# Attention with a key/value cache: 160 instead of 320 rows of wo go through the first five DMA engines

## Chip, core and metric

The kernel runs on one core of a Trainium2 chip. The metric is the device time of one execution in microseconds (us), lower being better. Before the change it is 189.44 us, the median of four runs (188.45, 188.66, 190.21 and 192.01 us).

A core has a matrix engine (PE, whose weight loads are listed apart as PEld), a vector engine (DVE), a scalar engine (ACT), GpSimd (POOL) and a synchronising engine (SP), which here issues the transfers. Sixteen DMA engines carry the transfers out.

## What is computed

```python
q = (x @ wq).reshape(B, Sq, Hq, Dh).transpose(0, 2, 1, 3)
k = jnp.repeat(k_cache, rep, axis=1)
v = jnp.repeat(v_cache, rep, axis=1)
scores = jnp.einsum("bhqd,bhkd->bhqk", q, k) * (Dh ** -0.5)
o = jnp.einsum("bhqk,bhkd->bhqd", softmax(scores), v)
return o.transpose(0, 2, 1, 3).reshape(B, Sq, Hq * Dh) @ wo
```

B is 8, Sq 4, D 512, Hq 32, Hkv 8 (so rep is 4), Sk 2048 and Dh 128; all in bf16. The caches k and v are 33.5 MB each (8 x 8 x 2048 x 128 x 2 bytes), wq and wo 4.2 MB each, and the output is 32 KB. The kernel reads 75.5 MB once and does little arithmetic on each byte.

## The kernel before

**Units.** Work goes in 32 units: four pairs of key/value heads (`p`) times eight batches (`b`), `units[u]`. A unit has 1 MB of k and 1 MB of v, each in one transfer into a tile of 128 partitions x 8 KB (`load_k`, L118, and `load_v`, L128). There are 7 k buffers and 6 v buffers. The loop at L488 takes step `n`: it transposes the keys of unit n on PE (L215) and copies them out on DVE and ACT (L216), computes the scores (L286) and the exponentials (L296) of unit n-1, transposes the probabilities on DVE (L306), and multiplies unit n-2 with its v (L343 for the last 20 units, L381 for pairs of the first 12).

**Transfers.** All loads are issued by SP, in the order of the list `loads` that is built at L153 to L163. The order begins: k of unit 0, wq (4 MB), x, then for u = 1, 2, ...: one `wo_e` transfer (as long as u is at most 8), k of unit u, v of unit u-2. `load_ready` (L165) issues from this list at the end of a step, as far as there are buffers. SP's transfers carry eight landing semaphores in rotation, so that transfer number m is issued when number m-8 has landed; a transfer has landed when the last of its DMA engines has. A tile of 128 partitions is spread evenly: each of the 16 DMA engines carries 8 partitions. A transfer of 5 partitions uses five DMA engines with one partition each. They are called the first five here.

**wo.** The 4096 rows of `wo` are used in four parts of 1024 rows, one for each `p`. Parts 1 to 3 are loaded at the end in eight transfers (L148), 128 partitions each. Part 0 is divided among three tiles (L52):

- `wo_e`: NE x WE = 40 x 8 = 320 rows. A partition holds 8 rows (8 KB). They come in eight transfers of five partitions each (`load_wo_e`, L133; 40 KB a transfer): transfers 0 to 3 fill partitions 0 to 19, transfers 4 to 7 partitions 32 to 51. The tile has 64 partitions, and the ones that no row fills are set to zero on POOL first (L178).
- `wo_m`: 128 x WM = 640 rows, five to a partition, and `wo_n`: the last WN = 64 rows, one to a partition. They are loaded near the end, just ahead of v of the last unit (L140 to L144).

**The output projection.** The attention output of part 0 is brought into the order of these rows: `to_tokens(0)` transposes it to token-major and copies it to `nat_sb` (L438 to L442; the columns for `wo_e` are copied as two blocks of 256, with columns of other rows filling the partitions that are zero in `wo_e`), and `to_wo_rows(0)` transposes it back, one transpose for each row slot (L459 to L463), into `oE`, `oM` and `oN`. `project(p, r0, n)` (L468) accumulates in PSUM (`out_ps`), two matmuls for each row slot. The `wo_e` slots are done in steps 14 to 17 (L531), the `wo_m` and `wo_n` slots one step before the last unit (L533). After the last unit come `to_tokens(2)`, `to_wo_rows(2)` and the projection of parts 1 to 3 (L536 to L543), then the copy to `out_sb` (L545) and two stores.

The tiles `pad0` and `pad` hold nothing: they only set where the tiles after them lie in SBUF.

Of the kernel before, what the change touches and what calls it, by code (L numbers as in the profile page):

```python
# [8 lines left out]
BF16 = mybir.dt.bfloat16  # L9
# [5 lines left out]
def kernel(  # L15
# [9 lines left out]
    nc = tc.nc  # L25

    B, Sq, D = x.shape
# [4 lines left out]
    T = B * Sq  # L32
# [8 lines left out]
    HP = 2 * rep  # L41
# [7 lines left out]
    DH = D // 2  # L49


    NE, WE, WM, WN = 40, 8, 5, 64  # L52
    assert NE * WE + 128 * WM + WN == HP * 128
    AX = mybir.AxisListType.X
    ADD = mybir.AluOpType.add
# [2 lines left out]
    const = ctx.enter_context(tc.tile_pool(name="const", bufs=1))  # L58
# [13 lines left out]


    pad0 = const.tile([128, 192], BF16, name="pad0")
    wo_e = const.tile([64, WE, D], BF16, name="wo_e")
    wo_n = const.tile([WN, D], BF16, name="wo_n")
    wo_m = const.tile([128, WM, D], BF16, name="wo_m")
    x_sb = const.tile([T, D], BF16, name="x_sb")
# [11 lines left out]
    oT = [const.tile([128, HP, len(ps), B, Sq], BF16, name=f"oT{ps[0]}") for ps in groups]  # L90
    out_sb = const.tile([2 * T, DH], BF16, name="out_sb")
    oP12 = const.tile([128, WR, 2, T], BF16, name="oP12")
    nat_sb = const.tile([2 * T, HP * 128 + 24 * WE], BF16, name="nat_sb")
    oP3 = const.tile([128, WR, T], BF16, name="oP3")
    oP = [None, oP12[:, :, 0, :], oP12[:, :, 1, :], oP3[:, :, :]]
    oE = const.tile([64, WE, T], BF16, name="oE")
    oM = const.tile([128, WM, T], BF16, name="oM")
    oN = const.tile([WN, T], BF16, name="oN")
    ident = const.tile([128, 128], BF16, name="ident")
# [3 lines left out]

    fold = const.tile([128, 2, 2, NQ], FP32, name="fold")
    ones = const.tile([128, 128], FP32, name="ones")
    pad = const.tile([128, 64], BF16, name="pad")
    probs = [const.tile([128, C, 2, HQ], BF16, name=f"probs{i}") for i in range(3)]

    units = [(p, b) for p in range(G2) for b in range(B)]
# [22 lines left out]

    def load_wo_e(i):  # L133

        hi, m = divmod(i, 4)
        rows = wo[: NE * WE, :].rearrange("(q r) j -> q r j", r=WE)
        a, b = hi * 32 + m, hi * NE // 2 + m
        nc.sync.dma_start(wo_e[a : a + 17 : 4, :, :], rows[b : b + 17 : 4, :, :])

    def load_wo_m():  # L140
        nc.sync.dma_start(wo_n[:, :], wo[HP * 128 - WN : HP * 128, :])
# [10 lines left out]
    nc.sync.dma_start(x_sb[:, :], x.flatten_outer_dims())  # L152
    loads = []  # L153
    for u in range(NU + KA):
        if 1 <= u <= 8:
            loads.append(("e", u - 1))
        if 0 < u < NU:
            loads.append(("k", u))
        if u == NU + KA - 2:
            loads.append(("m", 0))  # L160
        if u >= KA - 1 and u - KA + 1 < NU:
            loads.append(("v", u - KA + 1))
    loads.reverse()  # L163

    def load_ready(nk, nv):  # L165

        while loads:
            kind, u = loads[-1]
            if kind in "em":
                loads.pop()  # L170
                load_wo_e(u) if kind == "e" else load_wo_m()
                continue
            if u >= (nk + KB if kind == "k" else nv + VB):
                return
            loads.pop()
            (load_k if kind == "k" else load_v)(u)
# [6 lines left out]
    for e in range(2):  # L183
        for g in range(2):
            nc.vector.tensor_copy(
                out=pick[:, e, g, :], in_=ident[:, :].rearrange("d (k e) -> d e k", e=2)[:, e, :]
            )
    nc.vector.memset(q_bd[:, :, :, :, :, :, :], 0.0)
    for t in probs:
# [3 lines left out]
        out=by_q[:, :, :],  # L193
        in_=ident4[:, :].rearrange("p (g c q) -> p g q c", g=2, q=HQ),
# [4 lines left out]
    for c in range(2):  # L199
        nc.vector.tensor_copy(  # L200
            out=fold[:, c, :, :],
            in_=ident4[:, :].rearrange("p (u c q) -> p c u q", u=2, c=2)[:, c, :, :],
# [28 lines left out]
    for half in range(2):  # L231
        psq = psum_s.tile([4 * T, rep * Dh], FP32, tag="s", name="psq")
        for r in range(R):
            for k in range(4):
                n = (half * 4 + k) * rep * Dh
# [15 lines left out]
        for k in range(4):  # L251
            nc.vector.tensor_copy(  # L252
                out=qT_all[:, half * 2 + k // 2, :, k % 2 * rep : (k % 2 + 1) * rep, :],
                in_=qtp[:, :, k, :, :].rearrange("d h b s -> d b h s"),
            )
    for pp in range(0, G2, 2):
        for e in range(2):
# [9 lines left out]
            for g in range(2):  # L267
                rows = slice(g * 64, (g + 1) * 64)
                (nc.scalar.copy if g else nc.vector.tensor_copy)(
                    out=q_bd[rows, pp : pp + 2, e, :, :, g, :].rearrange("d p b g q -> d p (b g) q"),  # L270
                    in_=pse[rows, :, :, :, :].rearrange("d p b g q -> d p (b g) q"),
# [150 lines left out]
    nats = {}  # L422

    def to_tokens(n):
        rows = len(groups[n]) * T
        nat = psum_l.tile([rows, HP, 128], BF16, tag="l", name="nat")
        for h in range(HP):
            nc.tensor.transpose(
                nat[:, h, :], oT[n][:, h, :, :, :].rearrange("d p b s -> d (p b s)"), ident[:, :]
            )  # L430
        flat = nat[:, :, :].rearrange("t h d -> t (h d)")
        nats[n] = nat_sb[:rows, : HP * 128 + (n == 0) * 24 * WE]
        if n > 0:
            nc.vector.tensor_copy(out=nats[n][:, :], in_=flat)
            return

        w = 32 * WE
        nc.vector.tensor_copy(out=nats[0][:, :w], in_=flat[:, :w])  # L438
        nc.vector.tensor_copy(
            out=nats[0][:, w : 2 * w], in_=flat[:, NE // 2 * WE : NE // 2 * WE + w]  # L440
        )
        nc.vector.tensor_copy(out=nats[0][:, 2 * w :], in_=flat[:, NE * WE :])  # L442

    def to_wo_rows(n):
        rows = len(groups[n]) * T
        if n > 0:
            perm = psum_l.tile([128, WR, rows], BF16, tag="l", name="perm")
            by_row = nats[n][:, :].rearrange("t (q r) -> t r q", r=WR)
            for r in range(WR):
                nc.tensor.transpose(perm[:, r, :], by_row[:, r, :], ident[:rows, :rows])  # L450
            to = oP3[:, :, :] if n == 2 else oP12[:, :, :, :].rearrange("q r p t -> q r (p t)")
            nc.vector.tensor_copy(out=to, in_=perm[:, :, :])
            return

        perm = psum_l.tile([128, WE + WM + 1, T], BF16, tag="l", name="perm")
        w = 64 * WE
        by_row = nats[0][:, :w].rearrange("t (q r) -> t r q", r=WE)
        for r in range(WE):
            nc.tensor.transpose(perm[:64, r, :], by_row[:, r, :], ident[:T, :T])  # L459
        by_row = nats[0][:, w : w + 128 * WM].rearrange("t (q r) -> t r q", r=WM)  # L460
        for r in range(WM):
            nc.tensor.transpose(perm[:, WE + r, :], by_row[:, r, :], ident[:T, :T])
        nc.tensor.transpose(perm[:WN, WE + WM, :], nats[0][:, w + 128 * WM :], ident[:T, :T])  # L463
        nc.vector.tensor_copy(out=oN[:, :], in_=perm[:WN, WE + WM, :])
        nc.vector.tensor_copy(out=oE[:, :, :], in_=perm[:64, :WE, :])
        nc.vector.tensor_copy(out=oM[:, :, :], in_=perm[:, WE : WE + WM, :])

    def project(p, r0, n):  # L468
# [19 lines left out]
    for n in range(NU + A):  # L488
        w = n - A
# [16 lines left out]
        if w >= 0:  # L506
            p, b = units[w]
            if p in (1, 3) and b == 1:
                to_tokens(p // 2)
            if w >= NU - NS:  # L510
                values(w)
                if w % 2 == 0:
                    norms(w)
                finish(w)
            elif w % 2 == 1:
                values2(w - 1)
            if p in (1, 3) and b == 2:
                to_wo_rows(p // 2)
# [14 lines left out]
        if w == NU - 2:  # L533
            project(0, WE, WM + 1)

    to_tokens(2)  # L536
    project(1, 0, 4)
    to_wo_rows(2)
    project(1, 4, 4)
    project(2, 0, 4)  # L540
# [37 lines left out]
```

The softmax here doesn't subtract the row's maximum and nothing guards it: scores larger than these inputs give would overflow.

## Time and profile before

| | |
|---|---|
| median of four runs | 189.44 us (188.45 to 192.01) |
| the profiled execution's own time | 190.21 us |
| its span in the profile | 188.4 us |
| PE, PEld, DVE busy | 76%, 61%, 70% of the span |
| ACT, POOL busy | 33%, 2% |
| SP's DMA queue (q1): time of its packets, as a share of 16 DMA engines | 96.5% |
| read from HBM | 75.53 MB, 401 GB/s over the span |

The span runs from the first instruction to the last; 190.21 - 188.4 = 1.8 us of this execution's time lie around it. The profile's waits name what an engine stood still for. "DMA" as the one waited for means that data had not landed; "issue" is time in which the engine waited for nothing that the profile shows. Beside the page, the trace holds the start, duration and size of every DMA packet, and for each transfer up to 16 landing marks, one from each DMA engine that carried a part of it. The records do not name the DMA engine, but an engine can be followed from one transfer to the next by its place among the marks.

### The profile page before, as it was taken

To read this page: it belongs to the slowest core of one execution; us is meant where nothing else is said; L and a number is where in the kernel's file an instruction comes from. 1 tells how busy PE (TensorE), PEld (TensorE's weight loads), DVE (VectorE), ACT (ScalarE), POOL (GpSimd) and SP (SyncE) were. 2 spreads that over 40 slices of the span, in tenths; PEclk is the share of its full clock that TensorE was granted. 3 is DMA by queue.
4 is the path that set the end of the run, shared out by engine and by line. 5 is a ranking of instruction groups with operands and counts; after the bars stand their busy time and mean duration, and the time that the engine had idled before them with its cause. 6 is when DMAs were issued, how large, how long until landed. Compare 5 with 4: busy or idle time off the path is not lost.

```text
span 188.4 us, 4854 instructions
## 1 busy us (share of the span) xinstructions
PE 142.3 (76%) x2090; PEld 114.1 (61%) x2090; DVE 132.1 (70%) x260; ACT 62.4 (33%) x110; POOL 4.6 (2%) x9
## 2 busy tenths in 40 slices
PE   0704789978996959999687887767676787877693
PEld 0601248867775848888566666656565666766472
DVE  0840378979797778888787885878686887888220
ACT  2011147344533433444333333333333333335000
POOL 8000000000000000000000000000000000000000
PEclk9999999999999999999999999999999999999558
DMA  5999999999999999999999999999999999999970
GB/s 200 468 445 358 388 388 395 423 431 421 419 426 433 417 424 433 419 430 423 428 424 423 426 423 423 426 424 426 424 426 423 431 419 428 424 423 408 413 310 11
DMA packets 10980, 75.86 MB, mean 403 GB/s; under 512 B 1288, under 2 KB 1448, under 8 KB 2600
## 3 DMA queue, kind: packets, MB, share of 16 engines
q1 hardware_dynamic: 10912, 75.55, 96.5%
q8 instruction: 16, 0.26, 0.5%
q14 instruction: 4, 0.03, 0.0%
q10 hardware_dynamic: 48, 0.02, 0.0%
HBM read 75.53 MB, written 0.03 MB: 401 GB/s over the span
## 4 chain that ended last, share of the span: by engine, by line
DMA 76%; PE 14%; DVE 5%; ACT 2%; issue 1%; SPq 0%
DMA k_sb<-in_k_cache_dram 60%; DMA v_sb<-in_v_cache_dram 9%; DMA x_sb<-in_x_dram 7%; PE kp L215 4%; PE out_ps L480 3%; PE psq L236 2%; DVE probs L306 2%; PE s_ps L286 2%; DVE kt L216 1%; PE qtp L246 1%; PE perm L450 1%; ACT q_nat L243 1%; PE pse L260 1%; PE o_ps L343 1%; ACT kt L216 1%
## 5 line engine op out<-in xcount | busy, mean ns | idle before, releaser
L215 PE MATMUL kp<-ident,k_sb 128*128 128x128 f32 x512 | 71.1, 285 | 27.4 <-DMA k_sb<-in_k_cache_dram 25.5
L215 PEld LDWEIGHTS kp<-ident,k_sb 128*128 128x128 f32 x512 | 57.5, 145 | 38.1 <-issue 20.5
L216 DVE COPY kt<-kp 128x1024 bf16<-128x1024 bf16 x96 | 63.1, 686 | 23.7 <-PE kp L215 23.6
L306 DVE STREAM_TRANSPOSE probs<-s_sb 64x512 bf16<-64x512 bf16 x64 | 44.9, 702 | 0.6
L296 ACT ACTIVATE s_sb<-s_ps 128x512 bf16<-128x512 f32 x32 | 19.1, 597 | 69.4 <-PE s_ps L286 69.4
L216 ACT COPY kt<-kp 128x1024 bf16<-128x1024 bf16 x32 | 32.4, 1012 | 15.7 <-PE kp L215 15.7
L343 PE MATMUL o_ps<-probs,v_sb 128*128 128x32 bf16 x640 | 19.2, 177 | 2.6 <-DMA v_sb<-in_v_cache_dram 2.6
L343 PEld LDWEIGHTS <-v_sb 128*128 128x128 bf16 x640 | 18.5, 96 | 3.8 <-DMA v_sb<-in_v_cache_dram 3.4
L286 PE MATMUL s_ps<-kt,q_bd 128*32 128x256 bf16 x512 | 20.4, 276 | 0.0
L286 PEld LDWEIGHTS <-q_bd 128*32 128x32 bf16 x512 | 10.6, 95 | 5.5 <-issue 4.3
L381 PE MATMUL o_ps<-v_sb,probs 128*64 128x256 bf16 x192 | 11.6, 274 | 0.0
L381 PEld LDWEIGHTS <-probs 128*64 128x64 bf16 x192 | 10.0, 110 | 0.9 <-issue 0.8
L401 ACT ACTIVATE o_sb<-o_ps,r_sb 128x256 f32<-128x256 f32 x6 | 2.8, 474 | 11.9 <-DVE r_sb L399 11.9
L354 DVE TENSOR_TENSOR oT<-o_ps,r_sb 128x32 bf16<-128x32 f32 x20 | 3.8, 191 | 3.6 <-PE o_ps L343 3.0
L296 ACT ACTIVATION_READ_ACCUMULATOR s_sb<-s_ps 128x1 f32 x32 | 6.2, 194 | 0.0
L336 DVE RECIPROCAL r_sb<-l_ps 128x64 f32<-128x64 f32 x10 | 5.6, 557 | 0.3
L480 PE MATMUL out_ps<-wo_sb,oP 128*32 128x256 bf16 x48 | 5.6, 407 | 0.0
L252 DVE COPY qT_all<-qtp 128x128 bf16<-128x128 bf16 x8 | 1.2, 218 | 5.8 <-PE qtp L246 5.8
L410 PE MATMUL f_ps<-fold,o_sb 128*128 128x64 f32 x24 | 3.9, 283 | 1.7 <-ACT o_sb L401 1.6
L227 PE MATMUL xtp<-ident,x_sb 32*128 32x32 bf16 x4 | 0.3, 194 | 6.3 <-DMA x_sb<-in_x_dram 6.3
L410 PEld LDWEIGHTS f_ps<-fold,o_sb 128*128 128x128 f32 x24 | 3.1, 190 | 2.6 <-ACT o_sb L401 2.4
L243 ACT ACTIVATE q_nat<-psq 128x512 bf16<-128x512 f32 x2 | 1.2, 597 | 10.3 <-PE psq L236 10.3
(59 smaller groups left out, 65.6 us busy)
## 6 DMA issues: line engine op xcount, KB each, us to landing
k_sb<-in_k_cache_dram SPq DMA_DIRECT2D x32, 1024.0 KB, 19.6
v_sb<-in_v_cache_dram SPq DMA_DIRECT2D x32, 1024.0 KB, 14.2
wq_sb<-in_wq_dram SPq DMA_DIRECT2D x1, 4096.0 KB
wo_sb<-in_wo_dram SPq DMA_DIRECT2D x4, 512.0 KB
wo_sb<-in_wo_dram SPq DMA_DIRECT2D x4, 256.0 KB, 9.3
wo_m<-in_wo_dram SPq DMA_DIRECT2D x1, 640.0 KB, 16.7
wo_e<-in_wo_dram SPq DMA_DIRECT2D x8, 40.0 KB
wo_n<-in_wo_dram SPq DMA_DIRECT2D x1, 64.0 KB
```

Source lines behind the costliest of these rows:

```text
L215: nc.tensor.transpose(kp[:, j, :], k4[:, w : w + 128], ident4[:, :])
L216: (nc.scalar.copy if part == 3 else nc.vector.tensor_copy)(out=kt[(u, t)][:, half * JT // 2 : (half + 1) * JT // 2, :, :].rearrange("k j s ...
L236: nc.tensor.matmul(psq[k * T : (k + 1) * T, :], lhsT=xT_sb[:, r, :], rhs=wq_sb[:, r, n : n + rep * Dh], start=(r == 0), stop=(r == R - 1),)
L286: nc.tensor.matmul(s_ps[y * 32 : (y + 1) * 32, t * JT : (t + 1) * JT, :], lhsT=q_bd[:, p, e, b, y // 2, :, :], rhs=kt[(u, t)][:, :, y * 32 ...
L296: nc.scalar.activation(out=s_sb[:, :, :], in_=s_ps[:, :, :], func=EXP, accum_out=l_sbs[u][:, u % 2 : u % 2 + 1],)
L306: nc.vector.transpose(out=pr[rows, :, g, :], in_=s_sbs[u][rows, :, :].rearrange("q j s -> q (j s)"))
L336: nc.vector.reciprocal(r_sb[:, :, :], l_ps[:, :, :])
L343: nc.tensor.matmul(o_ps[:, :], lhsT=vs[u][:, c, :], rhs=pr[:, c, :, :].rearrange("s g q -> s (g q)"), start=(c == 0), stop=(c == C - 1),)
L354: nc.vector.tensor_tensor(out=oT[(p + 1) // 2][:, :, (p == 2) * 1, b, :], in0=o_pss[u][:, :].rearrange("d (h s) -> d h s", h=HP), in1=r_sb ...
L381: nc.tensor.matmul(o_ps[i * 64 : (i + 1) * 64, :], lhsT=probs[(u + i) % len(probs)][:, c : c + 2, :, :].rearrange("s c g q -> s (c g q)"), ...
L410: nc.tensor.matmul(f_ps[:, :, :].rearrange("d u q -> d (u q)"), lhsT=o_sbs[u][:, c, :], rhs=fold[:, c, :, :].rearrange("k u q -> k (u q)") ...
L480: nc.tensor.matmul(out_ps[half * T : (half + 1) * T, :], lhsT=o, rhs=w[:, half * DH : (half + 1) * DH], start=(p == 0 and r == 0), stop=(p ...
```

## The change

Part 0 of `wo` is divided differently: 20 x 8 = 160 rows in `wo_e` (four transfers of 40 KB instead of eight), 128 x 6 = 768 rows in `wo_m` (6 KB to a partition instead of 5 KB) and 96 rows in `wo_n` (96 partitions instead of 64). The sum of the rows, and of the bytes, is the same. `wo_e`, `oE` and their transposes have 32 partitions instead of 64. The columns for `wo_e` in `nat_sb` are one block instead of two, and `wo_m` has one row slot more, which is one transpose and two matmuls more. `pad` is 128 columns instead of 64, so that `probs` and everything behind it lie 1024 bytes further in each partition.

```diff
-    NE, WE, WM, WN = 40, 8, 5, 64
+    NE, WE, WM, WN = 20, 8, 6, 96
...
-    wo_e = const.tile([64, WE, D], BF16, name="wo_e")
+    wo_e = const.tile([32, WE, D], BF16, name="wo_e")
...
-    nat_sb = const.tile([2 * T, HP * 128 + 24 * WE], BF16, name="nat_sb")
+    nat_sb = const.tile([2 * T, HP * 128 + 12 * WE], BF16, name="nat_sb")
...
-    pad = const.tile([128, 64], BF16, name="pad")
+    pad = const.tile([128, 128], BF16, name="pad")
...
     def load_wo_e(i):
-        hi, m = divmod(i, 4)
         rows = wo[: NE * WE, :].rearrange("(q r) j -> q r j", r=WE)
-        a, b = hi * 32 + m, hi * NE // 2 + m
-        nc.sync.dma_start(wo_e[a : a + 17 : 4, :, :], rows[b : b + 17 : 4, :, :])
+        nc.sync.dma_start(wo_e[i : i + 17 : 4, :, :], rows[i : i + 17 : 4, :, :])
...
-        if 1 <= u <= 8:
+        if 1 <= u <= 4:
             loads.append(("e", u - 1))
...
         w = 32 * WE
         nc.vector.tensor_copy(out=nats[0][:, :w], in_=flat[:, :w])
-        nc.vector.tensor_copy(
-            out=nats[0][:, w : 2 * w], in_=flat[:, NE // 2 * WE : NE // 2 * WE + w]
-        )
-        nc.vector.tensor_copy(out=nats[0][:, 2 * w :], in_=flat[:, NE * WE :])
+        nc.vector.tensor_copy(out=nats[0][:, w:], in_=flat[:, NE * WE :])
...
-        w = 64 * WE
+        w = 32 * WE
...
-            nc.tensor.transpose(perm[:64, r, :], by_row[:, r, :], ident[:T, :T])
+            nc.tensor.transpose(perm[:32, r, :], by_row[:, r, :], ident[:T, :T])
```

## Prediction, made before the changed kernel was run

> **What bounds the kernel now.** I read the page first: the slices, the queues and the chain that ended last.
>
> ```profile
> span 188.4 us, 4854 instructions
> DMA  5999999999999999999999999999999999999970
> GB/s 200 468 445 358 388 388 395 423 431 421 419 426 433 417 424 433 419 430 423 428 424 423 426 423 423 426 424 426 424 426 423 431 419 428 424 423 408 413 310 11
> ...
> q1 hardware_dynamic: 10912, 75.55, 96.5%
> q8 instruction: 16, 0.26, 0.5%
> q14 instruction: 4, 0.03, 0.0%
> ...
> DMA 76%; PE 14%; DVE 5%; ACT 2%; issue 1%; SPq 0%
> ```
>
> From the second slice on the DMA engines are always busy, 96.5% of the span with SP's queue alone, and the chain is DMA for 76%. The queues q8 and q14 carry the engines' own instructions, 0.29 MB, on the same DMA engines. Then the waits of SP, which issues the loads:
>
> ```profile
> SPq L128 <- DMA v_sb<-in_v_cache_dram: 48.3, 22, 3.1
> SPq L118 <- DMA k_sb<-in_k_cache_dram: 44.1, 22, 2.1
> ```
>
> Columns: who waited, for what, us in total, times, longest. SP stands behind landings. So a transfer is issued as soon as the one eight places before it has landed, and "landed" is the time of its slowest DMA engine.
>
> Next, the windows view by stage (the last column is GB/s, the one before it the busy share of the DMA engines):
>
> ```profile
> core 0: us, PE busy (x) PEld busy (x) DVE busy (x) ACT busy (x) POOL busy (x), PEclk, DMA share, GB/s
> 16.00:31.00 15.00, 12.32 (x102) 6.37 (x103) 7.42 (x19) 5.34 (x10) 0.00 (x0) 1.00 1.02 389
> 33.00:53.00 20.00, 18.37 (x248) 15.18 (x249) 17.59 (x35) 9.40 (x17) 0.00 (x0) 1.00 1.01 425
> 55.00:105.00 50.00, 42.33 (x622) 35.13 (x620) 39.31 (x80) 18.89 (x34) 0.00 (x0) 1.00 1.01 426
> ```
>
> From 33 us on the rate is 425 GB/s whatever the compute does. From 16 to 31 us it is 389 at the same share. The packet records say the same: an 8 KB packet takes 309 ns, 16 x 8192 B / 309 ns = 424 GB/s, and 336 to 345 ns between 16.2 and 31.6 us, on all engines at once. What makes that stretch slow the profile does not show. It costs 6 transfers x 0.27 us = 1.6 us, about what separates the runs of 188.5 from that of 190.2.
>
> What decides is whether the sixteen DMA engines end together. The page has no row for it; the landing marks have. Each line below is one transfer, with the time of its issue and then its sixteen marks, in us after the first of them:
>
> ```
> k issued at   6.36: eleven from 0.00 to 0.20; 0.76 0.80 0.85 0.86 0.87  (behind two wo_e)
> k issued at  18.40: eleven from 0.00 to 0.22; 1.33 1.38 1.44 1.45 1.46  (behind four)
> k issued at  40.45: nine from 0.00 to 0.23; 1.52 1.62; 2.53 2.61 2.62 2.63 3.50  (behind eight)
> k issued at 123.89: 0.00 0.06 0.13 1.47 1.50 1.61 1.63 1.64 2.61 2.63 2.87 2.93 3.02 3.12 3.15 4.29
> v of unit 31, 160.70: 0.00 0.11 0.13 1.56 2.68 2.77 2.79 2.80 2.82 2.87 2.94 2.96 3.07 3.10 3.25 4.25
> ```
>
> Five engines fall back by 0.25 to 0.35 us with each `wo_e` transfer, 2.5 us with all eight: these are the first five. The others fall back by about 1.3 us at a time, one engine after another, each time that q8 fetches 16 KB of instructions (16 fetches, one every 10 us, 0.9 to 1.2 us a packet). One of the first five falls back further, to 3.50 and 4.29, right after 8 KB fetches of q14 at 44.55 and 108.59 us. No engine's packets have a hole between 16 and 180 us. So a late engine is late by work, not by waiting: it is 1.0 us behind the next at the end (4.25 - 3.25), and every landing waits for it.
>
> Last the tail, from the timeline (start, us, engine, line; in brackets the idle time before):
>
> ```profile
> 174.94 1.25 PE L480 MATMUL out_ps<-wo_m,oM 128*32 128x256 bf16 x10 [0.42 <-DMA wo_m<-in_wo_dram]
> ...
> 177.38 1.04 PE L343 MATMUL o_ps<-probs,v_sb 128*128 128x32 bf16 x32 [0.87 <-DMA v_sb<-in_v_cache_dram]
> 178.46 0.19 DVE L354 TENSOR_TENSOR oT<-o_ps,r_sb 128x32 bf16<-128x32 f32 x1 [2.99 <-PE o_ps L343]
> ...
> 181.12 4.22 PE L480 MATMUL out_ps<-wo_sb,oP 128*32 128x256 bf16 x40
> ...
> 185.38 0.36 ACT L545 CAST out_sb<-out_ps 64x256 bf16<-64x256 f32 x1 [12.32 <-PE out_ps L480]
> ```
>
> The end hangs on v of unit 31, landing at 177.34 us. After it PE has no hole longer than 0.4 us. From 181.12 its 40 matmuls go in pairs every 0.213 us (the page's last slices show PE's clock at 5 tenths). The last piece of wo lands at 184.82, and the last four matmuls start 0.11 us after it: both limits are nearly level.
>
> **The change, part by part.**
>
> *Four `wo_e` transfers fewer.* Each is one 8 KB packet on each of the first five, 309 ns; the marks say 0.25 to 0.35. The five moved from 1.33-1.46 (after four) to 2.50-2.63 (after eight), so four are worth 1.2 us on these five and nothing on the other eleven.
>
> *The rows come back in `wo_n` and `wo_m`, on all sixteen.* `wo_n`: 2 more 1 KB packets an engine at 46 to 62 ns, 0.1 us. `wo_m`: 8 packets of 6 KB instead of 5 KB (5 KB took 196 ns in the median), 8 x 38 ns = 0.3 us by size. Together +0.4 us on every engine, ahead of v of unit 31 in the queue.
>
> *Sum for that landing.* The late engine: 4.25 - 1.2 + 0.4 = 3.45. The next, if it is not of the first five: 3.25 + 0.4 = 3.65. The later of the two, 3.65, against 4.25 is -0.6 us; if the mark at 3.25 is one of the first five, it is -0.8. I take -0.7, which the tail passes on whole: PE's chain starts from this landing, and the landings of wo behind it shift equally (184.82 to about 184.1).
>
> A rule speaks against this. The Trainium skill, DMA: Bandwidth & Descriptors, section Bandwidth, says that the HBM side limits a load, at about 358 GB/s a core, before the DMA engines do. By that, moving bytes from five engines to sixteen changes nothing, since the bytes are the same: 0 us. The rows speak for the engines: 425 GB/s is above that limit, and when one engine stands for a fetch, the packets of the others stay at 309 ns instead of taking the free share. Only the stretch from 16 to 31 us looks like a shared limit. I follow the rows.
>
> Another would make more of it. The same page, section Anatomy of one DMA, gives every transfer a fixed cost of about 2 us; four fewer would be -8 us if it were paid in line. The marks show 0.3 us for a whole `wo_e` transfer, because seven others are under way: the fixed part is latency, and nobody waits for it.
>
> *Issue and semaphores.* SP issues four times fewer (0.70 us each). SP only waits, so this is worth nothing. The landing semaphores that these held between 21 and 41 us go to k and v transfers, issued up to 5 us earlier. The DMA engines have no hole there, so 0 too. One new wait may come: v of unit 6 could be issued at 35.5, when its semaphore is free, but its buffer is that of unit 0, which PE reads until 36.4 (L381). k of unit 9 is queued behind it on SP. Five transfers of 2.45 us are then still queued, 12 us of cover for a wait of 1 us.
>
> *PE, DVE, POOL.* One transpose more and one copy (0.27 us) less, with the copy behind it 160 columns longer (about +0.1 us of its 0.50), lie in steps in which PE waits for k (25.5 us in all). Two matmuls more, 0.21 us at the half clock, stand before those of unit 31: PE idles 0.87 us there now, and 0.87 - 0.21 stays as cover. Without it they would cost 0.21. The zeroing of `wo_e` keeps its length per partition, so its 3.50 us; SP's first `wo_e` waits 2.8 us for it. Were it half, k of unit 1 would be issued up to 1.8 us sooner, behind 4 MB of wq that occupy the engines until 15 us: 0.
>
> The sum is -0.7 us on a span of 188.4. The profiled execution took 190.21, 0.8 over the median, so it would become 189.5. From the median it is 188.7.
>
> **Rivals.** (1) The engines share one limit after all: nothing is won, 189.4. For it: the slow stretch. Against it: 425 GB/s and the constant 309 ns. (2) Slower: the engine at 4.25 is not one of the first five, or the fetches of q14 hit another engine this time. Then the last engine only takes on the 0.4 us of `wo_n` and `wo_m`, or 0.6 if the 1 KB packets of 96 partitions take twice the slowest of 64 (6 x 124 - 4 x 62 ns = 0.5 in place of 0.1, most of it beside other engines' work): 189.8 to 190.0. It decides where the first five are less than 0.4 us behind the rest without the change. Against it: the mark that reaches 3.50 and 4.29 comes out of the five. (3) The slow stretch lasts longer because the first five stand less apart. Each further transfer costs 0.27 us, so beyond three of them the change loses, and past ten it is over 1%: 191.5. Against it: the removed transfers are the fifth to eighth, which reach the engines at 35.5 us, after the stretch has ended. (4) The stretch is missing in most of the new runs: 1.6 us less, 187.1; that would be chance, not the change. (5) The change does not do what it says: 5 partitions going to other engines. The marks show five engines a transfer, so no.
>
> **Numbers.** My forecast 0.68; (1) 0.12; (2) 0.10; (3) 0.04; (4) 0.06. The forecast itself spans 188.0 to 189.4, since a median of few runs moves with how many of them had the stretch. Taking in (1) and most of (2), and the lower edge of the forecast with fewer slow stretches, I give 187.5 to 190.0. About 1%, 1.9 us, is what a measurement of this kernel can tell from no change; the working gives 0.4%. Faster by more than that needs (4) on top: 0.10. Slower needs (3) or a bad draw: 0.06. Within it 0.84.
>
> **What would show it.** In the new landing marks: the first five stop at 1.3 to 1.5 us instead of 2.5; the last mark of k in mid-run is 3.1 to 3.3 instead of 4.3, with one of the others as late as the first five's latest; `wo_n` and `wo_m` cost every engine 0.4 us; v of unit 31 lands 0.6 to 0.8 us earlier against the first marks of the run (the slow stretch taken out); PE still idles before L343 of unit 31. The forecast is wrong if the last mark stays at 4.3, if packets outside the slow stretch change from 309 ns, or if DMA engines show holes.

## The result, and the profile after

The changed kernel took 188.41 us in the median of 35 runs (187.65 to 199.27), the kernel before 189.78 us in 56 runs beside it (188.38 to 200.76). The ratio is 0.9956, with a 95% interval of 0.9931 to 0.9981: 0.8 us faster. The medians are of all runs; every ratio here leaves out, for both kernels, the runs that lie over 1.5% above the fastest of the same kernel. Run twice more beside others, the changed kernel came to 0.9964 (0.9928 to 1.0000) and 0.9950 (0.9928 to 0.9973). The forecast was 188.7 us, 0.7 us faster.

The lines of the page that answer to those shown of before:

```profile
span 188.6 us, 4855 instructions
...
DMA  6999999999999999999999999999999999999981
GB/s 250 417 445 374 386 386 389 387 387 401 422 427 426 422 429 422 426 429 422 427 424 424 426 426 420 429 426 420 426 427 419 434 420 427 424 424 400 418 351 47
...
q1 hardware_dynamic: 10904, 75.55, 97.1%
q8 instruction: 16, 0.26, 0.5%
q14 instruction: 4, 0.03, 0.0%
...
DMA 84%; PE 10%; DVE 2%; ACT 1%; issue 1%; SPq 0%
DMA k_sb<-in_k_cache_dram 64%; DMA v_sb<-in_v_cache_dram 9%; DMA x_sb<-in_x_dram 7%; PE kp L213 4%; DMA wo_sb<-in_wo_dram 4%; PE psq L234 2%; PE s_ps L284 1%; DVE probs L304 1%; PE qtp L244 1%; ACT q_nat L241 1%; PE pse L258 1%; DVE q_bd L2
```

The span is 188.6 us, not shorter than before (188.4). Read alone, the two spans would say that the change did nothing. The slices tell why: the stretch of some 387 GB/s, which covered the slices up to 33 us before, now goes on to the ninth slice and into the tenth, 45 us. The windows view shows the same (columns as before):

```profile
core 0: us, PE busy (x) PEld busy (x) DVE busy (x) ACT busy (x) POOL busy (x), PEclk, DMA share, GB/s
16.00:31.00 15.00, 12.30 (x92) 6.45 (x93) 6.79 (x18) 5.17 (x9) 0.00 (x0) 0.55 1.01 386
33.00:53.00 20.00, 18.37 (x241) 15.09 (x242) 17.58 (x33) 9.35 (x18) 0.00 (x0) 1.00 1.01 402
55.00:105.00 50.00, 42.33 (x626) 35.14 (x625) 40.24 (x80) 18.97 (x35) 0.00 (x0) 1.00 1.01 425
```

From 16 to 31 us the rates are alike (386 and 389). From 33 to 53 us it is 402 here against 425, and 425 again later. The packet records have 8 KB packets of 336 to 345 ns from 16.1 to 45 us here (324 ns just after a fetch had held one engine), and from 16.2 to 31.6 us before. The stretch comes in some runs and not in others, and in differing lengths. The granted PE clock has no part in it: it was 1.00 in the stretch before, 0.55 in the one after, and 0.56 in the same 15 us of the profile below, which has no stretch.

A later profile of the changed kernel, from another chip (run e11 below), happens to have no such stretch, so it is the one to be laid beside the prediction:

```profile
core 0: us, PE busy (x) PEld busy (x) DVE busy (x) ACT busy (x) POOL busy (x), PEclk, DMA share, GB/s
16.00:31.00 15.00, 12.32 (x96) 6.40 (x100) 6.95 (x18) 5.21 (x9) 0.00 (x0) 0.56 1.01 428
33.00:53.00 20.00, 18.37 (x244) 15.08 (x245) 17.57 (x33) 9.35 (x18) 0.00 (x0) 1.00 1.01 426
55.00:105.00 50.00, 44.08 (x669) 36.67 (x666) 42.07 (x84) 20.59 (x37) 0.00 (x0) 1.00 1.01 425
```

Its span is 186.1 us. The other two can be brought to the same footing, as an estimate that takes e11 as the measure. The foremost engine reaches the first landing mark of k of unit 5 at 34.71 us in e11 and at 36.29 before: 1.58 us of stretch before. For the profile after, two k transfers later, the first mark is at 44.52 in e11 against 47.06: 2.54 us. (This one is rougher: its foremost engine was 0.56 us ahead of e11's already at k of unit 0, at 4.75 against 5.31 us; before and e11 are level there.) Without the stretch the spans are 188.40 - 1.58 = 186.8 us before and 188.64 - 2.54 = 186.1 us after, the latter about e11's. The difference is 0.7 us, the forecast sum. The lowest times, which need no such estimate, say it too: 187.65 against 188.38.

The landing marks, in us after the first mark of each transfer, before and in e11:

```
                     before                                     changed (e11)
k of unit 5          ... 1.58 1.61 1.61 1.65 1.65 1.66          ... 1.30 1.36 1.39 1.39 1.42 1.61
k of unit 9          ... 1.57 2.50 2.57 2.61 2.63 3.42          ... 1.29 1.39 1.39 1.42 1.49 1.53 1.61 2.24
v of unit 31         ... 2.96 3.07 3.10 3.25 4.25               ... 2.74 2.75 2.77 2.84 2.91
issue of v 31        160.70                                     157.98
its last landing     177.34 (175.8 without the stretch)         175.21
```

The five stop at 1.30 to 1.42 us instead of 2.50 to 2.63, and the engine that had stood alone at 4.25 is now among the others. It is still held by the same two 8 KB fetches of q14 (45 and 106 us). At v of unit 31 all 16 engines land within 2.9 us of each other. The last mark of k in mid-run (k of unit 26) was 4.29 before; it is 2.99 in e11 and 3.31 in the profile after.

The tail of the profile after, from the timeline:

```profile
175.41 0.83 PE L475 MATMUL out_ps<-wo_m,oM 128*32 128x256 bf16 x12 [0.87 <-DMA wo_m<-in_wo_dram]
...
177.85 1.03 PE L341 MATMUL o_ps<-probs,v_sb 128*128 128x32 bf16 x32 [1.46 <-DMA v_sb<-in_v_cache_dram]
...
181.58 2.89 PE L475 MATMUL out_ps<-wo_sb,oP 128*32 128x256 bf16 x32
...
184.71 0.40 PE L475 MATMUL out_ps<-wo_sb,oP 128*32 128x256 bf16 x4 [0.24 <-DMA wo_sb<-in_wo_dram]
...
185.31 0.40 PE L475 MATMUL out_ps<-wo_sb,oP 128*32 128x256 bf16 x4 [0.20 <-DMA wo_sb<-in_wo_dram]
```

and of e11:

```profile
175.26 1.04 PE L341 MATMUL o_ps<-probs,v_sb 128*128 128x32 bf16 x32 [0.76 <-DMA v_sb<-in_v_cache_dram]
...
179.01 4.14 PE L475 MATMUL out_ps<-wo_sb,oP 128*32 128x256 bf16 x40
...
183.19 0.36 ACT L540 CAST out_sb<-out_ps 64x256 bf16<-64x256 f32 x1 [12.85 <-PE out_ps L475]
```

PE waits for v of unit 31 longer than before in the first (1.46 us) and about as long in e11 (0.76 against 0.87): the two added matmuls stay covered. In e11 the 40 last matmuls go through in one piece at a granted clock of 0.54, 4.14 us (4.22 at 0.50 before). In the profile after, at 0.75, they went faster than the last pieces of wo landed, and PE waited for each of the last two. Either way the end hangs on the last landings.

### The profile page after: what moved, and what is told of

Its sections match the earlier page's. It is cut to its first block, busy times and chain, and to the rows that moved or that the text cites. A ratio compares the mean times of both kernels' runs of the same rounds, so it can differ in the third digit from the quotient of the medians.

```text
span 188.6 us, 4855 instructions
## 1 busy us (share of the span) xinstructions
PE 143.8 (76%) x2093; PEld 115.4 (61%) x2093; DVE 131.8 (70%) x259; ACT 62.4 (33%) x110; POOL 4.6 (2%) x9
## 4 chain that ended last, share of the span: by engine, by line
DMA 84%; PE 10%; DVE 2%; ACT 1%; issue 1%; SPq 0%
DMA k_sb<-in_k_cache_dram 64%; DMA v_sb<-in_v_cache_dram 9%; DMA x_sb<-in_x_dram 7%; PE kp L213 4%; DMA wo_sb<-in_wo_dram 4%; PE psq L234 2%; PE s_ps L284 1%; DVE probs L304 1%; PE qtp L244 1%; ACT q_nat L241 1%; PE pse L258 1%; DVE q_bd L267 0%; DVE kt L214 0%; DVE qT_all L250 0%; PE perm L445 0%
## 5 line engine op out<-in xcount | busy, mean ns | idle before, releaser
L213 PE MATMUL kp<-ident,k_sb 128*128 128x128 f32 x512 | 73.4, 292 | 24.2 <-DMA k_sb<-in_k_cache_dram 22.0
L213 PEld LDWEIGHTS kp<-ident,k_sb 128*128 128x128 f32 x512 | 59.7, 149 | 35.3 <-issue 15.9
L284 PE MATMUL s_ps<-kt,q_bd 128*32 128x256 bf16 x512 | 21.7, 287 | 0.0
L475 PE MATMUL out_ps<-wo_sb,oP 128*32 128x256 bf16 x48 | 4.9, 337 | 0.5 <-DMA wo_sb<-in_wo_dram 0.4
```

The source lines that it names most:

```text
L213: nc.tensor.transpose(kp[:, j, :], k4[:, w : w + 128], ident4[:, :])
L284: nc.tensor.matmul(s_ps[y * 32 : (y + 1) * 32, t * JT : (t + 1) * JT, :], lhsT=q_bd[:, p, e, b, y // 2, :, :], rhs=kt[(u, t)][:, :, y * 32 ...
L475: nc.tensor.matmul(out_ps[half * T : (half + 1) * T, :], lhsT=o, rhs=w[:, half * DH : (half + 1) * DH], start=(p == 0 and r == 0), stop=(p ...
```

## The experiments

Eleven runs. The rival to the explanation by late engines ("theory A") was that small transfers cost by their number ("theory B"); further theories came up on the way. "Rows" are those of part 0 that go through the first engines. Ratios are to the kernel before, with the 95% interval; the lowest time is given because every profile with a stretch took longer than the lowest run of its kernel. The kernel before had lowest times of 188.33 to 188.42 in these jobs.

| run | rows, transfers | ratio | lowest us |
|---|---|---|---|
| changed | 160, 4 | 0.9956 (0.9931 to 0.9981) | 187.65 |
| e1 none | 0, 0 | 0.9972 (0.9934 to 1.0009) | 187.96 |
| e2 four of 80 KB | 320, 4 | 0.9988 (0.9954 to 1.0021) | 188.34 |
| e3 twelve | 480, 12 | 1.0075 (1.0042 to 1.0109) | 190.15 |
| e4 eight wide | 256 over eight engines, 4 | 0.9958 (0.9925 to 0.9992) | 188.11 |
| e5 eight of 60 KB | 480, 8 | 1.0002 (0.9963 to 1.0042) | 189.05 |
| e6 four at 64 | 160, 4 | 1.0072 (1.0036 to 1.0108) | 188.82 |
| e7 changed again | 160, 4 | 0.9964 (0.9928 to 1.0000) | 187.69 |
| e8 one nudge | 160, 4 | 0.9985 (0.9970 to 1.0001) | 187.81 |
| e9 two nudges | 160, 4 | 0.9983 (0.9968 to 0.9998) | 187.81 |
| e10 two on ACT | 160, 4 | 0.9966 (0.9925 to 1.0007) | 187.69 |
| e11 changed, third | 160, 4 | 0.9950 (0.9928 to 0.9973) | 187.78 |

### Number of transfers or bytes per engine: e1, e2

e1 takes `wo_e` and `wo_n` out; `wo_m` has all 1024 rows. e2 keeps four transfers but puts 16 rows in a partition. (Here and below, what follows from such a line, the sizes of tiles and of `pad` and the number of row slots, is left out at `...`.)

```diff
# e1
-    NE, WE, WM, WN = 20, 8, 6, 96
+    NE, WE, WM, WN = 0, 0, 8, 0
...
# e2
+    NE, WE, WM, WN = 20, 16, 5, 64
...
```

> No wo_e transfer at all: the 1024 rows of part 0 all come in one 128-partition transfer near the end (64 KB an engine). Theory A (each DMA engine ends by its own work, and the last one sets the time): the first five lose their 2.5 us, the eight engines that fetch PE's instructions stay at about 3.1 us after the first mark, and every engine takes 20 KB more than before the change, 0.8 us. 3.1 + 0.8 against 4.3: 0.4 us faster than before, ratio 0.998, and 0.4 us slower than the changed kernel. Rival B (each small transfer costs by being one more transfer, in issue and landing semaphores, about 0.1 us): eight fewer are worth twice what four were, ratio 0.991. In the marks, A: no group of five falls back together at the start, last mark of k in mid-run about 3.1.

> Four transfers as in the changed kernel, but 80 KB each (16 KB to a partition), so that 320 rows go through the first five DMA engines as before the change. Theory A (work per engine): same as before, ratio 1.000 within 0.002; the five fall back by 0.6 us with each transfer and stand 2.5 us behind after four; last mark of k in mid-run 4.2 to 4.4. Rival B (number of transfers): same as the changed kernel, ratio 0.9956, and a last mark of about 3.3.

e2 has the changed kernel's number of transfers and the old one's bytes, and its lowest time is the old one's (188.34 against 188.33; changed kernel 187.65). Its interval reaches down to 0.9954, so the ratio alone would not exclude theory B; the marks do. After two transfers the five stand at 1.22 to 1.59 us, after four at 2.17 to 2.58, and the last mark of k in mid-run is 4.30, as before the change (us after the first mark of each transfer):

```
e2, k of unit 2              ... 0.32 1.22 1.51 1.54 1.55 1.59
e2, k of unit 9              ... 1.57 2.17 2.57 2.57 2.58 3.42
e2, k of unit 21             ... 2.58 2.58 2.94 3.12 4.30
e1, k of unit 2              0.00 0.09 0.22 ... 0.50 0.51 0.57 0.73
e1, k of unit 21             ... 1.90 1.92 2.02 2.09 3.50
```

In e1 no group of five falls back, and the marks are the single fetches alone; yet without the 2.5 us of `wo_e` the last mark in mid-run is still 3.50. Theory A said about 3.1, B had nothing to say on it. Ratio 0.9972 against A's 0.998 and B's 0.991, which lies outside the interval. So theory B falls: taking the last four small transfers away as well gained nothing more, and by the lowest times lost 0.3 us. Why e1's last mark is 0.4 us above the forecast stays open.

### The slope: e3, e5, e6

e3 goes on to twelve transfers. Their partitions are 0 to 19, 32 to 51 and now 64 to 83.

```diff
# e3, against the kernel before
-    NE, WE, WM, WN = 40, 8, 5, 64
+    NE, WE, WM, WN = 60, 8, 4, 32
...
-        a, b = hi * 32 + m, hi * NE // 2 + m
+        a, b = hi * 32 + m, hi * NE // 3 + m
...
```

> Twelve transfers of 40 KB instead of eight, 480 rows through the first five. Theory A: the first five fall back by 3.7 us instead of 2.5, last mark of k in mid-run 5.5, and every engine has 10 KB less at the end (0.4 us): 0.8 us slower than before, ratio 1.004. Rival B: 0.4 to 0.8 us slower too, so this run gives the slope but does not tell the two apart. If DMA engines shared one limit (rival 1 of the prediction): ratio 1.000.

The marks came as expected (last mark 5.47 in mid-run), but the loss was twice theory A's: lowest time +1.8 us, and even the lower end of the interval is at 1.0042. The packet records show where: four times, from 54.3, 59.7, 65.3 and 70.8 us on, some 20 to 40 packets of 380 to 528 ns come together, each time as one of the last four `wo_e` transfers runs. All sixteen engines lose by it: the first marks of the k and v transfers, otherwise 2.45 us apart, are once 2.79 to 2.87 us apart at each of the four, and the last marks fall back as much on top of the 0.3 us of their own packet. The windows view catches the second:

```profile
core 0: us, PE busy (x) PEld busy (x) DVE busy (x) ACT busy (x) POOL busy (x), PEclk, DMA share, GB/s
59.50:60.50 1.00, 1.00 (x21) 0.77 (x22) 1.00 (x2) 0.34 (x1) 0.00 (x0) 1.00 1.08 360
61.00:63.00 2.00, 2.00 (x34) 1.80 (x33) 1.97 (x4) 1.01 (x1) 0.00 (x0) 1.00 1.03 426
```

The rate falls to 360 GB/s for that microsecond. Two readings were possible: too much spread, or those partitions. e5 has the same 480 rows in the old partitions, with 12 rows in each; e6 is the changed kernel with its four transfers moved.

```diff
# e5, against the kernel before
+    NE, WE, WM, WN = 40, 12, 4, 32
...
# e6, against the changed kernel
-        nc.sync.dma_start(wo_e[i : i + 17 : 4, :, :], rows[i : i + 17 : 4, :, :])
+        nc.sync.dma_start(wo_e[64 + i : 64 + i + 17 : 4, :, :], rows[i : i + 17 : 4, :, :])
...
```

> 480 rows through the first five, as with twelve transfers of 40 KB, but in eight transfers of 60 KB (12 KB to a partition) that fill the same partitions as before the change (0 to 19, 32 to 51). Twelve transfers measured 1.0075, where theory A expected 1.004; its last four, into partitions 64 to 83, fall together with packets of 0.4 to 0.5 us on all sixteen DMA engines. Theory A1 (the slope is that of the bytes on the first five; the excess comes from the partitions 64 to 83): 0.8 us slower than before, ratio 1.003 to 1.005, last mark of k in mid-run about 5.5, no long packets on all engines at once. Theory A2 (beyond some 4.5 us of spread the late engines hold up the issue for all, whatever the partitions): about 1.0075 as with twelve.

> The changed kernel with its four wo_e transfers into partitions 64 to 83 instead of 0 to 19; bytes, transfers and order unchanged. Theory A1 (such a transfer holds all engines for about 0.35 us): 4 x 0.35 = 1.4 us slower than the changed kernel, ratio to before 1.002 to 1.004, with long packets on all sixteen engines at the four places where the transfers run. Theory A2: no difference from the changed kernel, ratio 0.9956.

e5: last mark 5.60 us, no long packets on all engines, lowest time 0.7 us above before's, ratio 1.0002 with an interval up to 1.0042. That is A1's 0.8 us by the lowest times and excludes A2's 1.0075; the interval does not tell A1's 1.004 from no change. e6: 1.0072, by the ratios 2 us slower than the changed kernel on the same chip (e7, 0.9964), and by the lowest times 1.1 us (188.82 against 187.69), with not one byte or transfer more. Its long packets come at 17.7, 23.8 and 30.2 us, 31 to 39 of them each time, as its second to fourth `wo_e` transfers run; the first, at 15.5 us, has none. The window from 16 to 31 us:

```profile
core 0: us, PE busy (x) PEld busy (x) DVE busy (x) ACT busy (x) POOL busy (x), PEclk, DMA share, GB/s
16.00:31.00 15.00, 12.20 (x103) 6.34 (x104) 7.58 (x19) 5.41 (x10) 0.00 (x0) 1.00 1.02 357
```

357 GB/s, against 386 of the changed kernel with a stretch. e6's profile has a stretch as well, and a slower one: between the three places packets take 369 ns, and later 352, instead of 342. So the price of one such transfer isn't measured cleanly; the 1.4 us expected lie between the 1.1 and the 2. The Trainium skill, SBUF — State Buffer, section Door 1: The DMA port swizzle, says that partitions 64 and up go through other ports than 0 to 63. That these five engines then write into ports of others would be a reason for a slowdown of those. No run shows which port an engine writes to, nor why all sixteen slowed.

> The changed kernel itself, for a comparison with the two others on one chip. Ratio to before 0.995 to 0.997; last mark of k in mid-run about 3.3 once all the fetches of q14 have been; first five not further back than 1.4 us after the four wo_e.

e7 came as expected: last mark 3.05 to 3.19 in mid-run, the five at 1.27 to 1.55 us after four transfers.

### More engines for the early rows: e4

```diff
-    NE, WE, WM, WN = 20, 8, 6, 96
+    NE, WE, WM, WN = 32, 8, 6, 0
...
+        nc.sync.dma_start(wo_e[i : i + 29 : 4, :, :], rows[i : i + 29 : 4, :, :])
...
```

> Four transfers of 8 partitions (64 KB) instead of 5: 256 rows through the first eight DMA engines, 768 rows on all sixteen, no wo_n. Theory A, if the three engines that have been at the front all along (never held by a fetch) are the sixth to eighth: they take the work without being last, every engine has 6 KB less than in the changed kernel (0.25 us), ratio to before 0.994 to 0.995. If instead the engines that fetch PE's instructions are among the first eight, those go to 3.1 + 1.2 us and the ratio is about 1.000. The marks tell which: eight marks a wo_e transfer, and no engine left at the front, or three of them. Rival B: as the changed kernel, 0.9956.

A miss, but one that the marks explain. At v of unit 31 they are:

```
0.00 0.24 | 0.98 1.12 1.22 | 1.47 1.58 1.63 | 2.71 2.84 2.88 2.92 2.95 3.04 | 3.95 3.99
```

Eight engines fell back by 1.0 to 1.2 us, as they should. Two of them are also held twice by fetches of q8 (2 x 1.4) and are now last at 3.95 to 3.99. At the front remain two engines that took no `wo_e`. So of the three foremost engines only one is among the sixth to eighth. By lowest time the version is 0.5 us behind the changed kernel; its ratio, 0.9958, does not tell it from that one or from the 0.994 to 0.995 expected.

### The slow stretch: e8, e9, e10

In seven of the nine profiles to this point (all but e3's and e4's) a stretch began at about 16 us; the first three ended at 31.3, 45.4 and 53.3 us, in the microsecond in which a fetch of q8 or q14 held an engine, and so did the other four. But of the 20 fetches that fell into these stretches 13 did not end one: the packets fell to 324 ns for about a microsecond and went back to 342. The longer the stretch, the longer the run. In all profiles here but e6's, the run lay 0.1 to 0.4 us above the lowest of its kernel without a stretch, 0.7 with one up to 22 us (e9), 1.8 up to 31, 2.8 up to 45, 3.5 up to 53 and 4.3 up to 56 us. Of a run more than 5.3 us above the lowest of its kernel no profile is on record. The next two runs hold two engines on purpose: ACT issues a transfer of two partitions into a tile that nothing reads, after the first half of the queries (e8, 10 KB a partition), or after each half (e9, 5 KB a partition).

```diff
# e9, against the changed kernel; e8 has half < 1, and 10 in place of 5
+    nudge_sb = const.tile([2, 2, 5, D], BF16, name="nudge_sb")
...
         nc.scalar.mul(out=q_nat[:, half, :], in_=psq[:, :], mul=scale)
+        if half < 2:
+            nc.scalar.dma_start(
+                nudge_sb[:, half, :, :], wo[2 * 5 * half : 2 * 5 * half + 2 * 5, :].rearrange("(q r) j -> q r j", r=5)
+            )
```

> The changed kernel with one more transfer, of 2 partitions of 10 KB into a tile that nothing reads, issued by ACT on its own queue at about 18.7 us, so that two DMA engines are held once, as an instruction fetch holds one. In seven profiles the slow stretch (packets of 336 to 345 ns on all engines from 16.1 us) ended within 0.5 us of a fetch by q8 or q14. Theory L (the stretch is a lockstep of the engines that holding one engine breaks): it ends at 19 to 21 us, or does not outlast 21 us in the profile, and the median of the runs comes to within 0.7 us of the lowest run. Theory M (the ends have another cause, or only some fetches do it by chance): the stretch, where it appears, goes on to 31 us or beyond, and the median stays 0.7 us or more above the lowest. Either way the two engines are 0.4 to 1.2 us later, so the lowest time is 0 to 1.2 us above the changed kernel's 187.7.

> As the run before, but two transfers of 2 partitions of 5 KB, at about 18.7 and 21.9 us: two chances to break a lockstep. Theory L: stretch over by 22 to 23 us, median within 0.7 us of the lowest. Theory M: as the changed kernel, stretch to 31 us or beyond where it appears. Lowest time 0 to 1.2 us above 187.7.

All 44 runs of the two lie between 187.81 and 189.60 us. Of the kernel before, 14 of the 43 runs of the same job are over 190 us, up to 196.43; of the changed kernel, 14 of 35 in its first series and 10 of 22 in e7. e8's profile has no stretch. e9's has one and shows its end (ACT's part of the timeline; ACTq is the issue):

```profile
18.11 0.60 ACT L242 ACTIVATE q_nat<-psq 128x512 bf16<-128x512 f32 x1 [7.78 <-PE psq L235]
18.12 0.54 ACTq L244 DMA_DIRECT2D nudge_sb<-in_wo_dram  x1
21.25 0.60 ACT L242 ACTIVATE q_nat<-psq 128x512 bf16<-128x512 f32 x1 [2.54 <-PE psq L235]
21.26 0.24 ACTq L244 DMA_DIRECT2D nudge_sb<-in_wo_dram  x1
```

```profile
core 0: us, PE busy (x) PEld busy (x) DVE busy (x) ACT busy (x) POOL busy (x), PEclk, DMA share, GB/s
16.00:22.00 6.00, 4.43 (x38) 1.35 (x39) 0.72 (x5) 1.19 (x2) 0.00 (x0) 1.00 1.02 388
22.00:31.00 9.00, 7.91 (x65) 4.85 (x64) 6.51 (x13) 4.02 (x7) 0.00 (x0) 1.00 1.01 422
```

In the packet records, the first transfer's two 5 KB packets run at 21.91 us. The 8 KB packets take 342 ns until then, up to 378 ns from 22.05 to 22.4 us, and 309 to 315 ns from 22.65 us on: 388 GB/s before, 422 after. (So the stretch ended 0.7 us after the packets, not the 0.2 us that the expectation of e10 gives.) The stretch is thus no limit of that time of the program, since the same 22 to 31 us run at full rate here, and a transfer from another queue can end it. That the engines hold each other in it remains a guess. The price is 0.1 us in the lowest time and most of the gain by the ratio (0.9985 and 0.9983). The runs over 190 us, which the ratio leaves out, are missing: over all runs the mean is 188.5 us for both, against 190.0 and 190.5 for the changed kernel in its own two series and 190.3 for the one before on the same chip.

e10 tried it without an added byte: ACT issues the third and fourth `wo_e` transfers, one after the `q_nat` of each half.

```diff
-        if 1 <= u <= 4:
+        if 1 <= u <= 2:
             loads.append(("e", u - 1))
...
         nc.scalar.mul(out=q_nat[:, half, :], in_=psq[:, :], mul=scale)
+        load_wo_e(2 + half, nc.scalar)
```

> The changed kernel with its third and fourth wo_e transfers issued by ACT on its own queue, at about 18.7 and 21.9 us, instead of by SP in the order of its list; no byte is added. The two runs with an added ACT transfer had no run above 189.6 us, and in one of them the slow stretch ended within 0.2 us of that transfer's packets. Theory L (a transfer of another queue, cutting in on a few engines, breaks the stretch): no run above 190 us, stretch over by 26 us where it appears, lowest time as the changed kernel's 187.7, median at most 188.4, below both kernels' medians. Theory M (it was the added bytes on two engines that did it): long stretches and runs above 190 us come back, in 40% or so of the runs.

> The changed kernel itself, on the same chip as the run before it. Lowest time 187.6 to 187.8, about 4 runs in 10 above 190 us, ratio to before 0.995 to 0.997.

Here 3 of e10's 10 runs are over 190 us (190.48, 192.77 and 193.51), against 4 of 13 of the changed kernel beside it and 5 of 22 of the one before. The expectation of theory L fails for this form. Its one profile has no stretch (8 KB packets of 309 ns throughout), so whether these transfers would end one is not shown. The changed kernel itself came as expected. What the two nudges have that this one lacks (two engines instead of five, packets that are not 8 KB) stays open, as does what starts the stretch. It was not tried whether a nudge at a later or earlier time would do. The best median of one job is e10's 187.92, but with ten runs, three of them over 190 us, it isn't shown to beat the changed kernel (187.97 beside it).

## Why the prediction was right

- **What bounds the kernel.** Confirmed. The time follows the last of the sixteen DMA engines, and moving work between engines moves the time with the bytes unchanged: e2, e5 and the change itself against each other. The change is shown by the lowest times and the marks, and the ratios agree.
- **Four `wo_e` transfers, 1.2 us on the five.** Confirmed: from 2.50-2.63 to 1.30-1.42 us.
- **The returned rows, 0.4 us on every engine.** Too small. From v of unit 30 to v of unit 31 the foremost engine took 4.46 us before, and 4.99 and 5.08 in the two profiles after: 0.5 to 0.6 us.
- **The sum, -0.6 to -0.8 us at v of unit 31.** Without the stretch, 175.76 to 175.21: -0.55, at the edge of the range. The tail passed it on; the spans differ by 0.7, of which 0.1 lies behind the landing of the output. That the sum came out is in part luck, for two terms were off and nearly cancel: the foremost engine reached v of unit 31 in e11 0.8 us later than before instead of 0.4 (171.5 to 172.3 us, without the stretch), and the last engine stood 2.9 us behind it instead of the 3.25 that the marks of before left as the next.
- **The number.** The median fell by 1.4 us, more than the forecast 0.7, as 14 of 35 runs were over 190 us with the change and 28 of 56 without, which is chance as far as the runs show; the ratio and the lowest times have 0.8 and 0.7.
- **The rule of one shared limit.** Did not decide: outside the stretch packets stayed at 309 ns at 425 GB/s with the work shifted. The prediction read the page too narrowly: the same section Bandwidth says that a core gets about 358 GB/s when both cores of its pair load, and lists 425 for one alone. Inside the stretch the limit looks shared: after a fetch had held one engine at 32 us in the profile after, the others' packets went from 342 to about 324 ns and back.
- **The rule of a fixed cost for each transfer.** Taking away the other four as well (e1) gained nothing. The section that the prediction names speaks of transfers issued by GpSimd; these are issued by SP.
- **Rival 2, that the late engine isn't one of the first five.** Excluded by e2, which put the five back and with them the last mark.
- **Rivals 3 and 4, the stretch.** It was longer in the profile after and would have hidden the gain, had the spans alone been read. The reason given against rival 3 (the removed transfers reach the engines after the stretch has ended) holds for the profile before alone; in other profiles the stretch goes on to 45 to 56 us. That the stretch has nothing to do with the change is not shown run by run, but over all jobs 28 of 70 runs are over 190 us with the change and 92 of 230 before it, 4 in 10 each.
- **Covers.** PE's wait ahead of v of unit 31 stayed (0.76 and 1.46 us), so the two added matmuls cost nothing. The new wait came too: in e11 SP issued v of unit 6 only at 36.95 us, and k of unit 9 behind it, and their first marks still followed the ones before by 2.4 to 2.5 us.

## What to carry to other kernels

Where DMA is the bound, ask which of the sixteen engines lands last, not how busy they are on average: every landing here waited for the slowest, and landing marks show it. Extra bytes are free on an engine only up to the lateness of the next; here four 40 KB transfers were about level with the engines that fetch instructions, and eight were too many. Before a gain of half a per cent is read off two spans, look for a stretch in one of them in which the packets themselves are slower.

## What the runs showed of the hardware

- Instruction fetches shift the load of a DMA-bound kernel: 16 fetches of 16 KB each held one engine for about 1.3 us, eight engines twice, and the others never; 8 KB fetches of q14 held engines of the first five for 0.6 to 1.0 us.
- A 40 KB transfer of five partitions cost all engines when it went to partitions 64 to 83 (packets of 380 to 535 ns instead of 309, at seven of eight such transfers) and only its own five when it went to partitions 0 to 19 or 32 to 51.
- From about 16 us the engines could fall into a state of 336 to 345 ns for 8 KB, some 388 GB/s for all together, for 6 to 40 us; in every profile it ended as a transfer of another queue ran, though 13 of 20 fetches that fell into it did not end it. With small ACT transfers to two engines none of 44 runs was above 189.6 us, where 14 of 43 of the kernel before were above 190 us.
